# An attention and expert-routing kernel on one core: 64x64 products throughout the attention rounds, a new order of each round, and routing constants loaded two rounds earlier

## The chip, the cores and the metric

The kernel runs on one core of one Trainium2 chip. The metric is the device time of one execution in microseconds (us). TensorE is the matrix engine (PE in the profile; PEld is its loading of weights), VectorE is DVE, ScalarE is ACT, GpSimd is POOL, and SyncE (SP) issues most transfers.

## What is computed

For 8 batches and 8 heads, causal attention over 576 positions with a window of 128, head width 64 and a bias that falls linearly with distance; the result, transposed to 4608 tokens of 512 numbers, goes through a layer of 8 experts. Each token goes to one expert, in order of all the gate's logits, and each expert takes 576.

```python
scores = scale * np.matmul(q, k.transpose(0, 1, 3, 2))
mask = (rel >= 0) & (rel < window)
scores = np.where(mask, scores + bias[None], -1000000000.0)
attn = softmax(scores)                       # by row
x = (attn @ v).transpose(0, 2, 1, 3).reshape(4608, 512)
logits = x @ w_gate                          # one expert a token, 576 tokens an expert
out[mask] = np.maximum(x[mask] @ w1[e], 0.0) @ w2[e]
```

## The kernel before, in words

**Pairs and tiles.** The attention works on 32 pairs of heads (8 batches x 4 pairs, NPAIRS). The two heads of a pair lie on partitions 0 to 63 and 64 to 127. The 576 positions are nine blocks of 64. Tiles 0 to 3 hold two query blocks each; the block that is left over, the ninth, is put together for an even and the following odd pair and is called tile 4. A query block meets at most three key blocks, so a tile's scores are up to 192 columns wide.

**Rounds.** `attention` (L42) runs 32 rounds and a tail. What a round does, and in which order, is written out by hand in ROUND (L33), a list of words: a letter for the step, one for the tile (or half, or head), and which pair it serves, counted back from the round's number. `M21-0` is the minimum for tile 2, head 1 of this round's pair; `T3-2` the transposes of tile 3 of the pair two rounds back. The first round has a list of its own (ROUND0), and so has the end (TAIL, L38). Every instruction of these steps is kept in this order on its engine (`put`), so each engine walks its own part of the list in order, and waits when a step's input or buffer is not ready.

**The steps**, and their engines:

- S (`scores`, L127), TensorE: q times k, in two halves: units 2 and 3 (S0), and 0, 1 and 4 (S1). A head works on its own half of the array's rows. For tiles 1 to 4 each product is 64x64 (head h, query block r: four quarters of the array). Tile 0 is written as one product of 64x128 for each head (L150), since both its blocks see the same keys. The scores land in one of two buffers (`ps_s`, two copies).
- M (`least`, L157), VectorE: adds the bias, takes the row minimum of the negated scores. E (`exps`, L169), ScalarE: the exponential with its row sum.
- T (`turn`, L184), TensorE: transposes of 128x128 into one of two banks (`ps_t`). P (`turned`, L197): copies the bank to SBUF: ScalarE for tiles 1 and 2, VectorE for 0 and 3 (L210).
- A (`av`, L213), TensorE: probabilities times v, 64x64 products, into the tile x (`ps_x`, one copy). X (`copy_out`, L247): the two halves of x to the tile xT, one on VectorE and one on ScalarE, by the parity of the pair (L253).
- N (`natural`, L271), TensorE: turns xT back to natural order and forms the gate's logits in the same product (64 columns of identity and 8 of gate weights, 72). For each tile and head one product of 64x128 (L281), eight in all; in every second round the ninth block adds four of 64x64. Float32 products are two instructions each.
- L (`logit_shares`), D1 and D0 (`divide`), VectorE: scale by the reciprocal sums, which G (`sums`, GpSimd) and I (`inverse`, L262, VectorE) made. In the last two pairs D is done by ScalarE in sixteen small products (L326).
- V (`load_v`), Q (`load`, L63: the q and k of the pair two rounds ahead, behind the last product issued before it) and Z (`store`), SyncE.
- R1 to R3 (`route`, L410): slots in which one step at a time of the routing that can be done early is put on VectorE (and a few products on TensorE). They run the generators in `router.steps` in order; the first one there is `load_consts`.

**The constants.** In round 5 (CONST_AT, L479), where Q is done, the kernel starts `load_consts` (L430): a transfer of 337.5 KB into craw. The following R1 puts the first cast of it (to c_ones) on VectorE.

**After the attention** come the first routing phase and, expert by expert, two layers of products whose weights are loaded, split in two parts and multiplied; the other routing phases run beside them.

Of the kernel before, what the change touches and what calls it, by code (L numbers as in the profile page):

```python
# [5 lines left out]
F32 = mybir.dt.float32  # L6
# [10 lines left out]
E, DM, F, N = 8, 512, 1024, 4608  # L17
CAP = N // E
NP = H // 2
# [3 lines left out]
QKW, BMW, XW, GW = 1152, 1408, 72, 8  # L23
# [5 lines left out]
def parts(words):  # L29
    return [(w[0], w[1:-2], -int(w[-2:])) for w in words.split()]  # L30


ROUND = parts("""S1-0 V-1 Q+2 G-2 M00-0 M11-0 S0-0 E11-1 T0-2 E21-1 E10-1 M21-0 T1-2 E00-1 E20-1 P1-2 P0-2 A-3 R1-3 M40-0 M31-0 M41-0 M01-0  # L33
E30-1 X1-3 T3-2 E01-1 T2-2 X0-3 I-2 M10-0 R2-3 M30-0 M20-0 E40-0 E41-0 R3-3 P3-2 N-3 L-3 D1-3 E31-0 P2-2 D0-3 Z-3""")

ROUND0 = parts("S0-0 S1-0 Q+2 M20-0 E20-0 M30-0 E30-0 M21-0 E21-0 M31-0 E31-0 M00-0 E00-0 M10-0 E10-0 M01-0 E01-0 M11-0 E11-0")

TAIL = [parts("""V-1 E21-1 G-2 E30-1 E01-1 T0-2 T3-2 P3-2 E10-1 P0-2 E00-1 A-3 R1-3 T2-2 X1-3 X0-3 E20-1 T3-1 R2-3 R1-3 R2-3 N-3 R3-3 P3-1 D0-3 P2-2 T1-2  # L38
E11-1 G-1 P1-2 T2-1 D1-3 Z-3 T1-1 L-3 P2-1 T0-1 A-2 R1-2 P1-1 I-2 I-1 P0-1 R2-2 R3-2 X1-2 X0-2 R1-2 R2-2 A-1 X1-1 X0-1 N-2 L-2 N-1 L-1 D0-2 D1-2 Z-2 D1-1 D0-1 Z-1""")]


def attention(tc, pools, qk_in, v_in, rel_in, C, x_dram, L_sb, router):  # L42

    nc = tc.nc
    sb, ps_s, ps_t, ps_x = (pools[k] for k in ("attn", "ps_s", "ps_t", "ps_x"))
    ident, wn = C["ident"], C["wn"]
    state, bm, batch, late, done, made, next_time = {}, {}, {}, [], set(), [], []
    hs = [slice(64 * h, 64 * h + 64) for h in range(2)]
    HR = [(h, r) for r in range(2) for h in range(2)]
# [4 lines left out]
    def mm(out, w, a, start=True, stop=True):  # L54
        i = nc.tensor.matmul(out, w, a, start=start, stop=stop, skip_group_check=True)  # L55
        put(i)
        made[:] = [i]
# [5 lines left out]
    def load(n):  # L63

        if n < NPAIRS:
            b, p = divmod(n, NP)
            t = sb.tile([128, QKW], F32, name="qk", bufs=3)
            i = nc.sync.dma_start(t, qk_in[b, p])
            put(i)
            if n > 2:  # L70
                tc.add_manual_dep(i.ins, made[0].ins.name, AFTER, reason="one pair a round")
            state[n] = dict(q=t[:, 0:576], k=t[:, 576:1152])
# [36 lines left out]
    def keys(n, t, r):  # L109

        par = n // NP % 2
        qb = par + 2 * t + r if t < 4 else 8 - 8 * par
        if t == 0:
            return qb, 0, qb + 1
        return qb, max(0, qb - 2), min(3, qb + 1)
# [11 lines left out]
    def scores(n, half):  # L127
        half = int(half)
        st = state[n]
        q, k = st["q"], st["k"]  # L130
        if "u" not in st:
            st["u"] = sb.tile([128, 1792], F32, name="u", bufs=4)
            st["mn"] = sb.tile([128, 10], F32, name="mn", bufs=4)
            st["sm"] = sb.tile([128, 10], F32, name="sm", bufs=6)
        if half and n == 0:
            s = [bank() for _ in range(2)]
        else:
            two = banks(ps_x if half and n == 1 else ps_s)
            s = [two[:, 512 * h:512 * h + 512] for h in range(2)]
        st["s", half] = s  # L140
        for t in UNITS[half]:
            if t == 4 and n % 2 == 0:
                continue
            m, c = unit(n, t)[0:2]
            w = 64 * m
            if t == 0:

                qb = keys(n, 0, 0)[0]
                for h in range(2):
                    mm(s[h][:, c:c + w], q[hs[h], 64 * qb:64 * qb + 128], k[hs[h], 0:w])  # L150
                continue
            for h, r in HR:
                one = state[n - 1 + r] if t == 4 else st
                qb, kb, _ = keys(n, t, r)
                mm(s[h][hs[r], c:c + w], one["q"][hs[h], 64 * qb:64 * qb + 64], one["k"][hs[h], 64 * kb:64 * kb + w])
# [41 lines left out]
    def turned(n, t):  # L197
        t = int(t)
        st = state[n]
        if "PT" not in st:  # L200
            st["PT"] = sb.tile([128, 2048], F32, name="PT", bufs=3)
        if nines(n, t):
            c, w, dims = 0, 512, ()
        elif t:
            c, w, dims = 0, 192, ((256, 2),)
        elif n // NP % 2:
            c, w, dims = 64, 384, ()
        else:
            c, w, dims = 128, 128, ((192, 2),)
        copy = nc.scalar.copy if t in (1, 2) else nc.vector.tensor_copy  # L210
        put(copy(steps(st["PT"][:, 512 * t + c:512 * t + c + w], *dims), steps(st["pt", t][:, c:c + w], *dims)))  # L211

    def av(n):  # L213
# [33 lines left out]
    def copy_out(n, i):  # L247
        st = state[n]
        i = int(i)
        if "xT" not in st:  # L250
            st["xT"] = sb.tile([128, 640], F32, name="xT", bufs=3)
        w = 256 if i or not n else 384 if n == NPAIRS - 1 else 320
        copy = nc.vector.tensor_copy if n % 2 != i else nc.scalar.copy  # L253
        put(copy(st["xT"][:, 384 * i:384 * i + w], st["x"][:, 512 * i:512 * i + w]))  # L254

    def sums(n):
# [4 lines left out]

    def inverse(n):  # L262
        t = 4 + n % 2
        s = state[n]["rs"] = sb.tile([128, 5, 2], F32, name="rs", bufs=3)
        put(nc.vector.reciprocal(s[:, 0:t], state[n]["sd"][:, 0:2 * t].rearrange("q (t h) -> q t h", h=2)))

    def nine(n):
# [3 lines left out]
    def natural(n, which):  # L271


        st = state[n]
        N = st["N"] = banks(ps_s if n == NPAIRS - 1 else ps_x)
        xT = st["xT"]
        for t in range(4):
            g = t // 2
            o = 384 * g + 128 * (t % 2)
            for c in range(2):  # L280
                mm(N[:, 512 * c + XW * t:512 * c + XW * t + XW], xT[hs[c], o:o + 128], wn[hs[c], n % NP, g, :])  # L281
        k = nine(n)
        if k is not None:
            for c, r in HR:
                a = xT[hs[c], 256 + 64 * r:320 + 64 * r] if k == n else state[n - 1 + r]["xT"][hs[c], 256:320]
                mm(N[hs[r], 512 * c + 4 * XW:512 * c + 5 * XW], a, wn[hs[c], (k - 1 + r) % NP, 0, :])
# [130 lines left out]
    put(nc.scalar.copy(wn[hs[1], :, :, 0:64].rearrange("k p g c -> k (p g) c"), bc(ident[hs[1], 64:128].unsqueeze(1), [64, 2 * NP, 64])))  # L417
    for n in range(NPAIRS + len(TAIL)):
        if n == 1:
            wg = pools["pp"].tile([128, NP, 2, GW], F32, name="wg")  # L420
            nc.sync.dma_start(wg, C["wg_in"].rearrange("k (p o e) -> k p o e", p=NP, o=2))
        if n == 2:
            put(nc.scalar.copy(wn[:, :, :, 64:XW], wg))
        if 0 < n < NP:
            biases(n)
        for what, which, back in ROUND0 if n == 0 else ROUND if n < NPAIRS else TAIL[n - NPAIRS]:
            k = n - back
            if what == "Q":
                load(k)
                if n == CONST_AT:  # L430
                    router.steps.append(load_consts(tc, pools["c"], C["cst_in"], C, router.nc.vector))
                    next(router.steps[0])
            elif 0 <= k < NPAIRS and not (what in "ME" and ((what, which, k) in done or which[0] == "4" and k % 2 == 0)):
                done.add((what, which, k))
                if what in alone:
                    alone[what](k)
                else:
                    work[what](k, which)
        if n == 0:

            z = C["zero"].bitcast(F32)
            for i in range(IDLE):
                put(nc.tensor.matmul(C["idle"][hs[i % 2], 0:64], z[hs[0], 0:64], z[hs[0], 0:64], start=True, stop=True,
                                     skip_group_check=True))
# [34 lines left out]
CONST_AT = 5  # L479
# [731 lines left out]
def load_consts(tc, pool, cst, C, eng):  # L1211
    nc = tc.nc
    n = sum(w for _, w, _ in CONSTS)
    raw = pool.tile([128, n], F32, name="craw")
    tc.keep_in_program_order(nc.sync.dma_start(raw, cst))
    yield "hold"
    o = 0
    for k, w, dt in CONSTS:
        r = raw[:, o:o + w]
        if dt == F32:  # L1220
            C[k] = r
        else:
            if dt == BF:
                t = pool.tile([128, w], BF, name="c_" + k)
                eng.tensor_copy(t, r)
            else:
                t = pool.tile([128, w, dt], BF, name="c_" + k)
                eng.tensor_copy(t, bc(r.unsqueeze(2), [128, w, dt]))
            C[k] = t
            yield 0  # L1230
        o += w
# [170 lines left out]
```

## Time and profile before

| | us |
|---|---|
| three runs | 695.52, 696.99, 697.02 |
| their median | 696.99 |
| profiled execution, its own time | 698.88 |
| profiled execution, span of the core | 697.0 |
| TensorE's mean granted clock over the span | 0.973 of full speed |

The profile's times run from the span's start. Rounds begin where the scores begin, here by the pieces of the chain: round 5 at 29.28, round 6 at 43.64, round 7 at 52.27, round 31 at 202.52; at 228.80 the first product of the routing count that has to wait for all of the attention starts. An instruction of TensorE is listed with the time it takes from start to end; several overlap, so a group's length is not the sum of its members'. In a row of the timeline, the idle time of the engine before it and what ended it stand in brackets.

### The profile page before, as it was taken

What the parts mean: (1) busy time and instruction counts of PE and PEld (TensorE: products, weight loads), DVE (VectorE), ACT (ScalarE), POOL (GpSimd) and SP (SyncE); (2) the same over time, 40 slices, a digit from 0 to 9 for tenths busy, and PEclk for the clock granted to TensorE, in tenths of its full rate; (3) what the DMA queues carried; (4) which work ended last, traced back from release to release, by engine and by line L of the source; (5) the groups of instructions that cost most, each with busy time, mean ns of one, the idle gap of its engine ahead of it and who ended that gap; (6) DMA issues with size and microseconds to landing.
All of it is one profiled execution on the core that took longest, in us unless ns stands there. A gap on an engine that the chain in (4) does not pass through costs nothing.

```text
span 697.0 us, 17694 instructions
## 1 busy us (share of the span) xinstructions
PE 654.8 (94%) x6691; PEld 562.6 (81%) x6692; DVE 466.3 (67%) x1959; ACT 375.6 (54%) x1062; POOL 112.9 (16%) x183
## 2 busy tenths in 40 slices
PE   8969999999997499999999999999999999999995
PEld 5748878778776279889879878988988988988985
DVE  5648788788887789977849778794774724523310
ACT  6847888878874153433324526645645655644210
POOL 4001110110100020331412214014014014011011
PEclk9979999999999599999999999999999999999999
DMA  7426567556542360733614755555545565531001
GB/s 238 150 95 197 168 196 228 174 181 218 164 137 58 98 221 30 271 107 121 205 45 161 204 114 161 158 130 162 154 127 157 147 145 156 153 82 38 1 24 49
DMA packets 60637, 98.02 MB, mean 141 GB/s; under 512 B 27904, under 2 KB 39296, under 8 KB 60544
## 3 DMA queue, kind: packets, MB, share of 16 engines
q1 hardware_dynamic: 54656, 77.92, 37.4%
q0 software_dynamic: 5888, 18.88, 8.2%
q8 instruction: 55, 0.90, 0.5%
q14 instruction: 38, 0.31, 0.1%
HBM read 72.01 MB, written 18.87 MB: 130 GB/s over the span
## 4 chain that ended last, share of the span: by engine, by line
PE 79%; DVE 8%; ACT 3%; issue 3%; DMA 3%; another core or an unknown queue 1%; SPq 0%; POOL 0%; POOLq 0%; DVEq 0%; ACTq 0%
PE ph L1140 24%; PE x L55 12%; PE po L1168 10%; PE po L1169 10%; PE po L1171 8%; PE s L55 7%; PE pt L192 4%; DVE hl L1048 2%; DVE xT L254 2%; ACT xT L254 1%; DMA raw<-in_w_dram 1%; DMA craw<-in_cst_dram 1%; DVE hlo L1150 1%; PE m L686 1%
## 5 line engine op out<-in xcount | busy, mean ns | idle before, releaser
L1140 PE MATMUL ph<-xh,hl 128*128 128x288 f32 (+2 forms) x1024 | 190.4, 300 | 0.5
L1140 PEld LDWEIGHTS ph<-xh,hl 128*128 128x128 f32 x1024 | 155.9, 190 | 3.0 <-issue 1.8
L1168 PE MATMUL po<-hl,hh 128*128 128x512 f32 (+1 forms) x328 | 128.3, 391 | 0.0
L1169 PE MATMUL po<-hl,hh 128*128 128x512 f32 (+1 forms) x328 | 126.2, 385 | 0.0
L174 ACT ACTIVATE u<-u,mn 128x192 f32<-128x192 f32 (+2 forms) x288 | 124.5, 436 | 2.0 <-DVE mn L165 2.0
L1140 PE MATMUL ph<-xl,hl 128*128 128x288 f32 (+2 forms) x512 | 116.2, 299 | 0.0
L1145 ACT ACTIVATE hh<-ph 128x288 fp32r<-128x288 f32 (+2 forms) x128 | 46.6, 409 | 106.4 <-PE ph L1140 91.9
L1171 PE MATMUL po<-hl,hlo 128*128 128x512 f32 (+1 forms) x264 | 101.3, 384 | 0.0
L1048 DVE TENSOR_TENSOR hl<-raw,hl 128x512 fp32r<-128x512 f32 x128 | 85.2, 684 | 21.8 <-ACT hl L1046 21.7
L1180 POOL DMA_INDIRECT out_dram<-o,idx x40 | 41.0, 1024 | 279.9 <-ACT o L1175 212.4
L1140 PEld LDWEIGHTS ph<-xl,hl 128*128 128x128 f32 x512 | 84.7, 190 | 0.2 <-DVE xl L1119 0.2
L165 DVE CUSTOM_DVE_ANT_0 u<-s,bm 128x192 f32<-128x192 f32 (+2 forms) x278 | 80.4, 333 | 4.0 <-PE s L55 3.1
L1046 ACT CAST hl<-raw 128x1024 fp32r<-128x1024 f32 x64 | 66.1, 1051 | 27.2 <-DMA raw<-in_w_dram 19.5
L1168 PEld LDWEIGHTS po<-hl,hh 128*128 128x128 f32 x328 | 61.8, 188 | 11.2
L1169 PEld LDWEIGHTS po<-hl,hh 128*128 128x128 f32 x328 | 61.7, 188 | 11.3
L1150 DVE SCALAR_TENSOR_TENSOR hlo<-ph,hh 128x288 fp32r<-128x288 f32 (+2 forms) x128 | 49.2, 417 | 31.3 <-ACT hh L1145 30.5
L1175 ACT COPY o<-po 128x512 f32<-128x512 f32 (+1 forms) x33 | 18.9, 574 | 91.2 <-PE po L1171 72.3
L192 PE MATMUL pt<-ident_sb,u 128*128 128x128 f32 x368 | 57.1, 285 | 1.5 <-ACT PT L211 1.0
L1171 PEld LDWEIGHTS po<-hl,hlo 128*128 128x128 f32 x264 | 49.6, 188 | 9.9
L55 PE MATMUL s<-qk 64*64 64x192 f32 (+2 forms) x992 | 56.2, 330 | 1.6 <-DVE mn L165 1.6
L174 ACT ACTIVATION_READ_ACCUMULATOR u<-u,mn 128x1 f32 x288 | 55.1, 191 | 0.0
L55 PE MATMUL x<-wn_sb,xT 64*128 64x72 f32 (+1 forms) x616 | 39.9, 278 | 12.8 <-ACT xT L254 7.9
(261 smaller groups left out, 864.5 us busy)
## 6 DMA issues: line engine op xcount, KB each, us to landing
raw<-in_w_dram SPq DMA_DIRECT2D x64, 512.0 KB, 4.5
qk<-in_qk_dram SPq DMA_DIRECT2D x32, 576.0 KB, 5.3
v<-in_v_dram SPq DMA_DIRECT2D x32, 288.0 KB, 3.5
x<-xb SPq DMA_DIRECT2D x14, 512.0 KB
x<-xb SPq DMA_DIRECT2D x16, 64.0 KB
x<-xb SPq DMA_DIRECT2D x4, 256.0 KB, 2.3
g<-x,idx POOLq DMA_INDIRECT x40
out_dram<-o,idx POOLq DMA_INDIRECT x40
```

The source lines that it names most:

```text
L55: i = nc.tensor.matmul(out, w, a, start=start, stop=stop, skip_group_check=True)
L165: put(nc.vector.tensor_tensor_reduce(out=weights(n, t, h), in0=s[h][:, c:c + 64 * m].rearrange("q (j k) -> q j k", k=64), in1=bm[n % NP][: ...
L174: put(nc.scalar.activation(u, u, AF.Exp, bias=st["mn"][:, i:i + 1], scale=-1.0, accum_out=st["sm"][:, i:i + 1]))
L192: put(nc.tensor.transpose(steps(ps[:, c:c + 64], (w, 2)), u[:, o + 128 * j:o + 128 * j + 128], ident))
L1046: self.last = nc.scalar.copy(hl[:, 0, :], raw)
L1048: nc.vector.tensor_tensor(hl[:, 1, c:c + 512], raw[:, c:c + 512], hl[:, 0, c:c + 512].bitcast(F32), ALU.subtract)
L1140: nc.tensor.matmul(pp[t], w[:, a, j, fo:fo + 128], x[:, j, cut[t]:cut[t + 1]], start=(i == 0), stop=(i == 11))
L1145: self.acted = nc.scalar.activation(o, pp[t], AF.Relu)
L1150: nc.vector.scalar_tensor_tensor(d, pp[t][:, c0:c1], 0.0, o[:, c0:c1].bitcast(F32), ALU.max, ALU.subtract)
L1168: nc.tensor.matmul(out, a, wh, start=(f == 0), stop=False)
L1169: nc.tensor.matmul(out, a, wl, start=False, stop=(f == 7 and t == 4))
L1171: nc.tensor.matmul(out, hl[:, f, 128 * t:128 * t + 128], wh, start=False, stop=(f == 7))
```

## The change

It does five things. The eight 64x128 products of N become sixteen of 64x64, in fours that use the four quarters of the array. Tile 0's scores are done like the other tiles', in 64x64 products. ROUND and TAIL are written anew: S0 follows S1 at once; the exponentials of tile 3 and the copy P0 move to the next round; I serves the pair three rounds back; T goes 3, 1, then A, then 2, 0; X0 comes right behind A and R1, and X1 near the end. The copies P1, P2 and X0 are VectorE's and P0, P3 and X1 ScalarE's, in all rounds. The constants' transfer is issued in round 3, while the steps that cast them still enter the list in round 5. The reciprocals' tile has six copies in place of three.

```diff
-ROUND = parts("""S1-0 V-1 Q+2 G-2 M00-0 M11-0 S0-0 E11-1 T0-2 E21-1 E10-1 M21-0 T1-2 E00-1 E20-1 P1-2 P0-2 A-3 R1-3 M40-0 M31-0 M41-0 M01-0
-E30-1 X1-3 T3-2 E01-1 T2-2 X0-3 I-2 M10-0 R2-3 M30-0 M20-0 E40-0 E41-0 R3-3 P3-2 N-3 L-3 D1-3 E31-0 P2-2 D0-3 Z-3""")
+ROUND = parts("""E30-2 S1-0 V-1 Q+2 S0-0 I-3 M41-0 E31-2 G-2 M01-0 P0-3 M21-0 T3-2 M20-0 E21-1 M10-0 E20-1 E10-1 T1-2 E11-1 M00-0 P1-2 M11-0 M40-0 P3-2 A-3 R1-3 X0-3
+E41-0 E40-1 T2-2 E00-1 M31-0 R2-3 M30-0 E01-0 T0-2 P2-2 X1-3 R3-3 N-3 D1-3 L-3 D0-3 Z-3""")
-TAIL = [parts("""V-1 E21-1 G-2 E30-1 E01-1 T0-2 T3-2 P3-2 E10-1 P0-2 E00-1 A-3 R1-3 T2-2 X1-3 X0-3 E20-1 T3-1 R2-3 R1-3 R2-3 N-3 R3-3 P3-1 D0-3 P2-2 T1-2
-E11-1 G-1 P1-2 T2-1 D1-3 Z-3 T1-1 L-3 P2-1 T0-1 A-2 R1-2 P1-1 I-2 I-1 P0-1 R2-2 R3-2 X1-2 X0-2 R1-2 R2-2 A-1 X1-1 X0-1 N-2 L-2 N-1 L-1 D0-2 D1-2 Z-2 D1-1 D0-1 Z-1""")]
+TAIL = [parts("""V-1 E11-1 E00-1 P0-3 T0-1 E21-1 T0-2 P0-1 P0-2 E20-1 T1-2 E31-2 T2-2 E30-2 G-2 P2-2 E30-1 E31-1 P1-2 I-3 A-3 R1-3 X1-3 T2-1 R2-3 T3-2 E40-1 E10-1 G-1
+R1-3 X0-3 P2-1 R2-3 I-2 N-3 R3-3 D0-3 P3-2 L-3 T3-1 D1-3 Z-3 T1-1 A-2 R1-2 P3-1 P1-1 R2-2 X0-2 R3-2 I-1 R1-2 X1-2 R2-2 A-1 X0-1 N-2 X1-1 N-1 L-2 L-1
+D0-2 D1-2 Z-2 D1-1 D0-1 Z-1""")]
+
+ON_VECTOR = {(0, "P1"), (1, "P1"), (0, "P2"), (1, "P2"), (0, "X0"), (1, "X0")}
...
-            if t == 0:
-
-                qb = keys(n, 0, 0)[0]
-                for h in range(2):
-                    mm(s[h][:, c:c + w], q[hs[h], 64 * qb:64 * qb + 128], k[hs[h], 0:w])
-                continue
...
-        copy = nc.scalar.copy if t in (1, 2) else nc.vector.tensor_copy
+        copy = nc.vector.tensor_copy if (n % 2, f"P{t}") in ON_VECTOR else nc.scalar.copy
...
-        copy = nc.vector.tensor_copy if n % 2 != i else nc.scalar.copy
+        copy = nc.vector.tensor_copy if (n % 2, "X%d" % i) in ON_VECTOR else nc.scalar.copy
...
-        s = state[n]["rs"] = sb.tile([128, 5, 2], F32, name="rs", bufs=3)
+        s = state[n]["rs"] = sb.tile([128, 5, 2], F32, name="rs", bufs=6)
...
-            o = 384 * g + 128 * (t % 2)
-            for c in range(2):
-                mm(N[:, 512 * c + XW * t:512 * c + XW * t + XW], xT[hs[c], o:o + 128], wn[hs[c], n % NP, g, :])
+            for c, r in HR:
+                o = 384 * g + 128 * (t % 2) + 64 * r
+                mm(N[hs[r], 512 * c + XW * t:512 * c + XW * t + XW], xT[hs[c], o:o + 64], wn[hs[c], n % NP, g, :])
...
+                if n == CONST_AT - 2:
+                    consts = load_consts(tc, pools["c"], C["cst_in"], C, router.nc.vector)
+                    next(consts)
                 if n == CONST_AT:
-                    router.steps.append(load_consts(tc, pools["c"], C["cst_in"], C, router.nc.vector))
-                    next(router.steps[0])
+                    router.steps.append(consts)
```

## Rows read from the trace of the kernel before

**Rows 1.** The page's chain that ended last, share of the span by engine.

```profile
PE 79%; DVE 8%; ACT 3%; issue 3%; DMA 3%; another core or an unknown queue 1%; SPq 0%; POOL 0%; POOLq 0%; DVEq 0%; ACTq 0%
```

**Rows 2.** Windows by stage: busy us (and count) of PE, PEld, DVE, ACT, POOL; PEclk; DMA.

```profile
29.28:43.64 14.36, 7.41 (x129) 6.03 (x126) 5.54 (x31) 6.07 (x26) 0.20 (x1) 0.83 0.45 144
43.64:52.27 8.63, 8.40 (x111) 6.28 (x112) 5.03 (x27) 4.29 (x18) 0.20 (x1) 0.69 0.22 70
52.27:202.52 150.25, 146.20 (x2751) 119.44 (x2751) 125.08 (x666) 124.10 (x507) 14.58 (x60) 1.00 0.58 188
202.52:228.80 26.28, 19.55 (x382) 16.22 (x380) 19.42 (x91) 14.51 (x60) 2.07 (x8) 0.96 0.27 80
```

**Rows 3.** Timeline of SyncE's issues, 14 to 36 us: start, length, instruction.

```profile
18.46 0.33 SPq L68 DMA_DIRECT2D qk<-in_qk_dram  x1
...
24.33 0.33 SPq L68 DMA_DIRECT2D qk<-in_qk_dram  x1
...
32.28 0.45 SPq L1215 DMA_DIRECT2D craw<-in_cst_dram  x1
```

**Rows 4.** Timeline of all engines, 26 to 44 us.

```profile
39.30 0.23 DVE L521 CAST c_ones<-craw 128x128 bf16<-128x128 f32 x1 [7.56 <-DMA craw<-in_cst_dram]
...
41.22 2.43 PE L55 MATMUL x<-wn_sb,xT 64*128 64x72 f32 x24 [6.96 <-ACT xT L254]
```

**Rows 5.** Timeline of TensorE in rounds 14 and 15, 101.8 to 121.5 us.

```profile
108.54 1.63 PE L55 MATMUL s<-qk 64*128 64x128 f32 x28
110.10 0.88 PE L192 MATMUL pt<-ident_sb,u 128*128 128x128 f32 x6
...
113.49 1.11 PE L55 MATMUL x<-wn_sb,xT 64*128 64x72 f32 x16 [0.24 <-DVE xT L254]
114.44 1.90 PE L55 MATMUL s<-qk 64*128 64x128 f32 x36
...
119.65 1.40 PE L55 MATMUL x<-wn_sb,xT 64*128 64x72 f32 x24
120.98 0.81 PE L55 MATMUL s<-qk 64*128 64x128 f32 x8
```

**Rows 6.** TensorE's 64x64 groups in narrow windows; then durations by source line, min/median/max ns.

```profile
121.40 1.21 PE L55 MATMUL s<-qk 64*64 64x192 f32 x24
...
120.70 0.36 PE L55 MATMUL x<-wn_sb,xT 64*64 64x72 f32 x8
...
L55 PE MATMUL s<-qk x992: 216/323/683, 5.4 to 203.8; 64*64 64x192 f32 x163, 64*128 64x128 f32 x12, 64*128 64x192 f32 x12, 64*64 64x64 f32 x12
...
L55 PE MATMUL x<-wn_sb,xT x616: 222/272/482, 22.3 to 223.5; 64*128 64x72 f32 x124, 64*64 64x72 f32 x30
```

**Rows 7.** VectorE by line and shape, 52.27 to 202.52: count, busy us, mean ns, idle before.

```profile
L211 DVE COPY PT<-pt 128x384 f32<-128x384 f32 x25 | 13.9, 554 | 1.3
L211 DVE COPY PT<-pt 128x512 f32<-128x512 f32 x12 | 8.2, 684 | 0.0
...
L254 DVE COPY xT<-x 128x320 f32<-128x320 f32 x12 | 5.9, 492 | 15.0 <-ACT xT L254 15.0
...
L211 DVE COPY PT<-pt 128x256 f32<-128x256 f32 x12 | 5.1, 424 | 0.0
```

**Rows 8.** Timeline of VectorE behind natural order of round 13, with a ninth block.

```profile
108.68 0.28 DVE L299 TENSOR_TENSOR Lp<-x,rs 128x64 f32<-128x64 f32 x1
...
109.76 0.28 DVE L165 CUSTOM_DVE_ANT_0 u<-s,bm 128x128 f32<-128x128 f32 x1
...
109.97 0.35 DVE L165 CUSTOM_DVE_ANT_0 u<-s,bm 128x192 f32<-128x192 f32 x1
110.24 0.08 DVE L165 DVE_READ_ACCUMULATOR2_ANT mn<- 128x1 f32 x1
```

**Rows 9.** Timeline of ScalarE and TensorE at the end of the tail.

```profile
224.54 1.75 ACT L326 ACTIVATE xb<-x,rs 128x64 f32<-128x64 f32 x8 [2.00 <-PE x L55]
...
228.80 0.31 PE L521 MATMUL m<-OH,ind 128*128 128x16 bf16 x5 [3.75 <-ACT xb L326]
```

## The prediction

> **What bounds the kernel now.** I read the chain that ended last first [rows 1]: TensorE carries 79% of it. The windows by stage [rows 2] say where that leaves room. From 228.80 on (routing, then the experts' layers) nothing is edited, so those 697.0 - 228.8 = 468.2 us stay. The attention before falls into four pieces: round 5 (14.36 us), round 6 (8.63), the 24 rounds from 7 to 30 (150.25, so 6.26 each), and round 31 with the tail (26.28). In the 24 rounds TensorE is busy 146.20 of 150.25, VectorE 125.08 and ScalarE 124.10. So TensorE sets the pace, but with only 17% of room on each of the other two: what it gains can be kept only until one of them, or a ring through all three, takes over.
>
> **The constants.** Their load is issued at 32.28 [rows 3], in round 5, and the cast that reads them stood on VectorE's ordered queue until 39.30, 7.56 us idle; with that queue the copies of xT stood, and TensorE idled 6.96 us until 41.22 [rows 4]. Afterwards the granted clock is 0.69 over round 6 (full before, half for part of it) [rows 2]. Rounds 5 and 6 took 14.36 + 8.63 = 22.99 us where two ordinary ones take 12.52: the load costs **10.5 us**. Issued in round 3 it stands on SyncE's queue behind the q/k load of 18.46; between it and the next q/k load, at 24.33 [rows 3], there is one v load, wanted three rounds later, which it delays by its own 0.45 us of issue. From issue to cast it took 39.30 - 32.28 = 7.02 us; from 18.8 it would land at about 26, and the cast is not wanted before round 5's A, at some 32. I take all of the 10.5; its bounds are 0 (still late) and 10.5.
>
> **Natural order in 64x64.** In round 14 the sixteen 64x128 instructions take 113.49 to 114.44, 0.95 us until the scores begin; in round 15, with eight 64x64 ones of the ninth block behind, 119.65 to 120.98, 1.33 [rows 5]. Sixteen in 1.11 us, less the 0.27 that one lasts [rows 6], start as eight pairs 0.12 us apart. The change makes thirty-two of them, in eight fours on the four quarters of the array. What a four costs is bounded by two rows [rows 6]: the ninth block's eight instructions of the same 72 columns, two fours, all start within 0.14 us (0.36 less the 0.22 that a short one lasts), entering the mode included; six fours of 192 columns start within 1.21 - 0.32 = 0.89 us, five steps of 0.17, also with the entry, which by columns is 0.065 for 72. I take 0.065, since of the ninth block only one step, the one with the entry, can be seen, and 0.05 for the entry: 8 x 0.065 + 0.05 = 0.57 without a ninth block, 10 x 0.065 + 0.05 = 0.70 with one. That saves 0.38 in even rounds and 0.63 in odd ones. If a four cost 0.113 (the 0.14 less start offsets), nothing would be saved in even rounds and 0.15 in odd ones.
>
> **Tile 0's scores.** Today they and the change of mode take 120.98 to 121.40, 0.42 us [rows 5, 6]. Two fours of 128 columns are 2 x 0.17 x 128/192 = 0.23. Saved: about 0.2, plus the entry that is no longer paid twice, 0.23 in all.
>
> A rule of the Trainium skill speaks against this part: "TensorE: Matmul & The Clock Gate", section "Wait — 56ns, not 53.3ns?", has the starts of matmuls never closer than some 25 ns, however narrow; by it (an estimate) N would take 0.80 and 1.00 and the sum would end some 7 us higher, near 673. The rows disagree: the ninth block's eight start within 0.14 us, 0.02 each [rows 6].
>
> **A round of TensorE** then is: even (108.54 to 114.44 now, 5.90 [rows 5]): scores 1.56 - 0.23, transposes and A 110.10 to 113.49, 3.39, of which 0.24 is waiting for xT, natural 0.57: 5.29, or 5.05 without the wait. Odd (114.44 to 120.98, 6.54): 6.54 - 0.63 - 0.23 = 5.68, with 0.2 of waiting in it. The mean is 5.27 without waits.
>
> **The other engines.** Copies P1, P2 and X0 go to VectorE, P0, P3 and X1 to ScalarE. VectorE gives up 24 of 554 ns, 12 of 684 and 12 of 424, and 12 xT copies of 256 columns (priced as P's 256, 424 ns); it takes 36 of 554, 12 of 684 and 12 xT of 492 [rows 7]. That is +1.6 and +0.8 us over 24 rounds, so 125.08/24 + 0.1 = 5.31 us a round; ScalarE falls by about 0.08 from 5.17. VectorE's floor is now as high as TensorE's.
>
> **The ring.** In the new order VectorE's queue runs, once natural order has ended: L, D1 and D0 (at a round's end, so they overlap the next scores), I, the minima M up to M40, P1, R1, X0; ScalarE's X1 follows X0 (the two are in series today, the row of X0 waits 15.0 us for ScalarE's [rows 7]); then natural order again. For an odd round: natural 0.86 to its last end and 0.1 to L; L to the first M 109.76 - 108.68 = 1.08; I 0.13; eight M at 110.24 - 109.97 = 0.27 from start to start [rows 8], some narrower, 2.1; P1 0.55; a router step 0.1; X0 0.49, X1 0.37, three hops of 0.05: 5.9. An even one, with six M and no ninth block, 5.0, beneath its TensorE sum. So odd rounds become VectorE's (6.0 with slips), even ones stay TensorE's (5.2): **5.60 a round**, 0.66 less, times 24 is **15.8 us**. Bounds: 5.31 (22.8 us) and 5.95 (7.4).
>
> The other moves cost nothing on the path. E30 and E31 start a round later, but ScalarE has them done before the scores end, ahead of T3. P0 comes after them, and T1, which wants its bank, stands behind all scores; if ScalarE ran a microsecond late, T3 and T1 would wait that long. S0 right behind S1 wants M31 and M30 of the round before, which precede P2. G on GpSimd and I move together; GpSimd is idle. The larger ring of rs tiles is memory only. The q/k load stays behind S1.
>
> **Early rounds and tail.** Rounds 5 and 6, once ordinary, gain 0.66 each; rounds 3 and 4 are partly ScalarE's, 0.3 each: 1.9. Round 31 gains 0.66. In the tail two natural-order groups of 1.3 us and one of 0.95 shrink by 1.6 in all. The closing products of ScalarE now start 2.0 us after its last copy, at 224.54, and the routing count waits for their end, 228.80 [rows 9]; with N-2 ahead of X1-1 they start about 1 us sooner. Against this stand three more exponentials left for the tail, 3 x 0.44. I take 0.66 + 1.6 + 0.7 = **3.0**, bounds 1 and 5.
>
> **Sum.** 10.5 + 15.8 + 1.9 + 3.0 = 31.2. The profiled execution took 698.88 us (span 697.0), 1.9 above the median of 696.99; 698.88 - 31.2 = 667.7, and as a median **665.8**.
>
> **Rivals.**
> - *VectorE's floor is reached*: the ring slips into the even rounds' slack and rounds take 5.31: 7.0 less, 659. For it: the order differs from round to round only by two minima. Against: an in-order queue at its floor has no idle at all. 0.13.
> - *The small products keep a distance by instruction, not by four.* The nearest rows give 0.02 an instruction (0.14/7, the ninth block) and 0.039 (0.89/23, the scores, 192 columns) [rows 6]: thirty-two take 0.64 to 1.25 us. In the middle, 0.03, N is 0.96 and 1.2, as with fours of 0.113: 0.4 to 0.5 more in each round, on TensorE and in the ring, rounds of about 5.95 and a smaller tail: 677. Against: in the ninth block the step between the fours holds the entry too. 0.06. (Such a distance is what the section of the Trainium skill named above states.)
> - *The ring runs later than its sum*: ScalarE's E41, E40, E00 and E01 stand before X1; if the M's they follow are late, N waits and rounds take 5.9 to 6.0: 674. For it: ScalarE at 5.09 of 5.60 us has little room left. Against: in the sum X1 is wanted 1.5 us after their last M. 0.07.
> - *The constants still come late*, because three loads at once are slower than today's: all 10.5 lost, 676. For it: the load shares the queues with q/k and v; against: 5 us of cover. 0.03.
> - *Slower: the ring pays full durations.* If each M cost 0.35 + 0.08 [rows 8] with no overlap and each hop 0.2, the ring would be about 7.9 in odd and 6.4 in even rounds, 7.2: 0.94 over today, 22.5 more in 24 rounds against 13.5 saved elsewhere: 706. It decides once rounds exceed some 6.8. Against: the M's start 0.27 apart in the rows. 0.02.
>
> My forecast has 0.69. What a measurement of this kernel can tell from no change is about 0.3%, 2.1 us; only the last rival, and half a percent of mishap, lie at or above that: faster 0.97, same 0.01, slower 0.02. The forecast's own range is 661 to 671; the rivals on both sides stretch it to 657 and 677.
>
> **What would show it.** The cast of c_ones has no wait, and the clock is 1.00 in rounds 5 and 6. Natural order is a row of x32 or x40 that lasts 0.8 to 0.95. No s matmul has the form 64*128. Rounds 7 to 30 take 134 us, odd ones near 6.0, even near 5.2, VectorE busy some 95%, and TensorE waits for X1 before N in odd rounds alone. It is wrong if the rounds stay over 5.9, if a four takes 0.1, or if the stage after the count changes length by over 2 us.

## The result and the profile after

The changed kernel takes **668.11 us** (median of 4 runs, 666.87 to 668.95); the kernel before took 697.0 beside it (4 runs, 695.52 to 697.4). The ratio is 0.9588, 95% interval 0.9567 to 0.9609. The forecast was 665.8, the range 657 to 677. The profiled execution took 668.95 us, with a span of 666.8.

The windows by stage of the kernel after answer to [rows 2]: rounds 5 and 6, rounds 7 to 30, round 31 with the tail, and everything from the routing count on.

```profile
29.04:34.88 5.84, 5.62 (x153) 4.72 (x149) 5.55 (x30) 5.17 (x24) 0.20 (x1) 1.00 0.67 220
34.88:40.27 5.39, 5.16 (x136) 4.27 (x131) 5.20 (x29) 4.73 (x21) 0.20 (x1) 1.00 0.54 193
40.27:175.36 135.09, 128.15 (x3230) 106.95 (x3225) 125.38 (x666) 119.58 (x505) 14.59 (x60) 1.00 0.65 209
175.36:199.77 24.41, 17.22 (x461) 14.59 (x454) 18.79 (x91) 16.08 (x67) 2.21 (x9) 0.97 0.29 87
199.77:666.80 467.03, 446.17 (x2916) 395.62 (x2916) 292.83 (x1036) 204.14 (x366) 91.63 (x89) 0.98 0.42 127
```

Rounds 5 and 6 fell from 14.36 and 8.63 us to 5.84 and 5.39, at the full clock. The 24 rounds fell from 150.25 to 135.09 us, 5.63 each: odd ones last 5.81 to 5.98, even ones 5.25 or 5.39, but for round 30 with 6.06 (6.79 before). TensorE is busy in 95% of them, VectorE in 93%. The stage behind the count is 1.2 us shorter. The chain that ended last has moved only by a little towards VectorE [rows 1]:

```profile
PE 78%; DVE 13%; ACT 3%; issue 2%; another core or an unknown queue 1%; DMA 1%; SPq 0%; POOL 0%; POOLq 0%; DVEq 0%; ACTq 0%
```

SyncE's issues in round 3 (start, length, instruction), for [rows 3], and VectorE's timeline in round 5, for [rows 4]:

```profile
18.89 0.33 SPq L71 DMA_DIRECT2D qk<-in_qk_dram  x1
19.26 1.14 SPq L1214 DMA_DIRECT2D craw<-in_cst_dram  x1
20.44 0.43 SPq L81 DMA_DIRECT2D v<-in_v_dram  x1
...
24.36 0.33 SPq L71 DMA_DIRECT2D qk<-in_qk_dram  x1
```

```profile
32.66 0.22 DVE L520 CAST c_ones<-craw 128x128 bf16<-128x128 f32 x1
```

The cast has no wait in front of it, and the next q/k load leaves at 24.36 as it did at 24.33.

The v load behind the constants' issue leaves 20.44 - 18.89 = 1.55 us after the q/k load in front of it; it was 0.37 in the kernel before.

Now two rounds, an even and an odd one, in the timeline of all engines: A, the copies X0 (VectorE) and X1 (ScalarE), N, and the scores that follow. The brackets tell how long the engine was idle in front, and what ended it.

```profile
104.01 1.55 PE L58 MATMUL x<-PT,v 64*64 64x192 f32 x48
...
105.65 0.49 DVE L251 COPY xT<-x 128x320 f32<-128x320 f32 x1 [0.28 <-PE x L58]
...
106.17 0.37 ACT L251 COPY xT<-x 128x256 f32<-128x256 f32 x1 [0.42 <-DVE xT L251]
...
106.60 0.73 PE L58 MATMUL x<-wn_sb,xT 64*64 64x72 f32 x32 [0.34 <-ACT xT L251]
...
107.15 1.70 PE L58 MATMUL s<-qk 64*64 64x128 f32 x40
...
111.44 0.49 DVE L251 COPY xT<-x 128x320 f32<-128x320 f32 x1 [0.22 <-PE x L58]
...
111.97 0.37 ACT L251 COPY xT<-x 128x256 f32<-128x256 f32 x1 [0.64 <-DVE xT L251]
...
112.39 0.86 PE L58 MATMUL x<-wn_sb,xT 64*64 64x72 f32 x40 [0.19 <-ACT xT L251]
```

Natural order takes 107.15 - 106.60 = 0.55 us until the scores begin, where sixteen 64x128 products took 0.95 [rows 5]. Inside a four the instructions start 0.007 us apart; from one four to the next it is 0.063, and 0.11 for the first step. In front of it TensorE waits for X1 in the even round too. X1 begins 0.03 us behind the end of X0 (105.65 + 0.49), and X0 itself waited for the end of A. So A, X0, X1 and N stand one behind the other, and VectorE had idled 0.28 and 0.22 us before X0: it was ready before TensorE was. X0 starts 0.05 to 0.09 us behind the end of A in 20 of the 24 rounds; in rounds 13, 21 and 29 it starts 0.21 to 0.22 behind it with no idle time of VectorE in front, so there VectorE was the later one.

The waits up to the count (engine and what it waited for: us in total, times, longest):

```profile
ACT xT L251 <- DVE xT L251: 16.4, 27, 0.8
...
PE x L58 <- ACT xT L251: 8.8, 29, 0.8
DVE xT L251 <- PE x L58: 4.6, 19, 0.4
```

TensorE's groups by shape in rounds 7 to 30 (count, busy us, mean ns, idle before) show that no product with 64*128 is left, for scores or natural order:

```profile
L58 PE MATMUL s<-qk 64*64 64x192 f32 x721 | 34.6, 323 | 0.0
...
L58 PE MATMUL x<-wn_sb,xT 64*64 64x72 f32 x864 | 19.0, 228 | 6.9 <-ACT xT L251 6.9
L58 PE MATMUL s<-qk 64*64 64x128 f32 x96 | 4.8, 269 | 0.0
```

The end of the tail, in the timeline of all engines, answers to [rows 9]:

```profile
194.52 0.96 PE L58 MATMUL s<-wn_sb,xT 64*64 64x72 f32 x40
195.53 1.74 ACT L323 ACTIVATE xb<-x,rs 128x64 f32<-128x64 f32 x8 [0.70 <-PE s L58]
...
199.77 0.31 PE L520 MATMUL m<-OH,ind 128*128 128x16 bf16 x5 [4.29 <-ACT xb L323]
```

ScalarE's closing products wait 0.70 us where they waited 2.00; the count still waits for their end.

### The profile page after: what moved, and what is told of

Its sections match the earlier page's. It is cut to its first block, busy times and chain, and to the rows that moved or that the text cites. A ratio compares the mean times of both kernels' runs of the same rounds, so it can differ in the third digit from the quotient of the medians.

```text
span 666.8 us, 19019 instructions
## 1 busy us (share of the span) xinstructions
PE 627.3 (94%) x7331; PEld 544.2 (82%) x7332; DVE 466.9 (70%) x1959; ACT 370.9 (56%) x1062; POOL 116.2 (17%) x183
## 4 chain that ended last, share of the span: by engine, by line
PE 78%; DVE 13%; ACT 3%; issue 2%; another core or an unknown queue 1%; DMA 1%; SPq 0%; POOL 0%; POOLq 0%; DVEq 0%; ACTq 0%
PE ph L1139 25%; PE po L1167 10%; PE x L58 10%; PE po L1168 10%; PE po L1170 8%; PE s L58 6%; PE pt L189 3%; DVE xT L251 2%; DVE hl L1047 2%; ACT xT L251 2%; DVE u L162 1%; DVE hlo L1149 1%; PE pg L1080 1%; PE m L685 1%
## 5 line engine op out<-in xcount | busy, mean ns | idle before, releaser
L1179 POOL DMA_INDIRECT out_dram<-o,idx x40 | 42.9, 1073 | 276.5 <-ACT o L1174 214.8
L1056 POOL DMA_INDIRECT g<-x,idx x40 | 42.6, 1066 | 63.0 <-DVE L L520 24.6
L189 PEld LDWEIGHTS pt<-ident_sb,u 128*128 128x128 f32 x368 | 39.8, 140 | 13.0 <-issue 8.5
```

The source lines that it names most:

```text
L189: put(nc.tensor.transpose(steps(ps[:, c:c + 64], (w, 2)), u[:, o + 128 * j:o + 128 * j + 128], ident))
```

## The experiments

A table first, for reading the sections below; all stages are from the profiled executions, in us, "rounds" being 7 to 30 and "tail" round 31 to the count. Each stage is counted from the first score product of its first round (the changed kernel's rounds from 40.09 to 175.36, so 135.27, where the window above has 135.09). Before and b_const, whose rounds 7 to 30 hold the same work, agree there within 0.01 us. The kernel before ran beside each group of runs on the same chip.

| kernel | median | before beside it | ratio, 95% interval | rounds 3 to 6 | rounds | tail |
|---|---|---|---|---|---|---|
| before | 697.0 | | | 35.00 | 150.23 | 26.47 |
| after | 668.11 | 697.0 | 0.9588 (0.9567 to 0.9609) | 22.36 | 135.27 | 24.42 |
| b_const | 687.11 | 696.47 | 0.9871 (0.983 to 0.9912) | 24.52 | 150.22 | 26.47 |
| b_nat | 682.55 | 696.47 | 0.9808 (0.9756 to 0.986) | 31.71 | 140.94 | 25.80 |
| b_tile0 | 689.54 | 696.47 | 0.9897 (0.9856 to 0.9939) | 33.57 | 145.31 | 26.29 |
| b_order | 697.65 | 696.47 | 1.0015 (0.9992 to 1.0038) | 33.09 | 152.93 | 25.65 |
| a_oldorder | 665.15 | 692.46 | 0.9605 (0.9574 to 0.9636) | 22.06 | 134.21 | 25.57 |
| a_dve | 666.06 | 692.46 | 0.9628 (0.9589 to 0.9667) | 22.40 | 137.58 | 24.43 |
| a_dve2 | 663.74 | 692.46 | 0.959 (0.9552 to 0.9629) | 22.35 | 135.74 | 24.44 |
| a_pe | 672.57 | 692.46 | 0.9713 (0.9682 to 0.9745) | 23.66 | 142.24 | 24.43 |
| a_lsplit | 666.52 | 696.15 | 0.9581 (0.9548 to 0.9614) | 22.36 | 135.62 | 24.50 |
| a_two | 661.02 | 696.15 | 0.9498 (0.9466 to 0.953) | 21.80 | 132.50 | 23.89 |
| a_two_old | 661.82 | 696.15 | 0.9503 (0.9466 to 0.9539) | 21.17 | 133.28 | 24.83 |

The chips differ by some 4 us, and the long stage behind the count varies from one execution to the next (461 to 468 us in these profiles, with nothing edited there), so medians are compared within a group, and parts of a round by stage.

### One part of the change at a time, in the kernel before

**b_const**: the constants alone.

```diff
+                if n == CONST_AT - 2:
+                    consts = load_consts(tc, pools["c"], C["cst_in"], C, router.nc.vector)
+                    next(consts)
...
-                    router.steps.append(load_consts(tc, pools["c"], C["cst_in"], C, router.nc.vector))
-                    next(router.steps[0])
+                    router.steps.append(consts)
```

> The kernel before with one edit: the constants' transfer is issued in round 3 and cast in round 5 as before. Theory (the load was late by its own flight, and all of that and of the half clock behind it comes back): 10.5 us less, 686 to 687, the cast of c_ones without a wait, the clock 1.00 over rounds 5 and 6. Rival (three transfers at once are slower, the cast still waits): less than 5 us back, 692 to 697, with a wait left in front of the cast.

Measured: rounds 3 to 6 take 35.00 - 24.52 = 10.5 us less, and the rounds behind do not change at all. The windows of rounds 3 to 6 and 7 to 30 of this kernel:

```profile
17.64:42.16 24.52, 24.07 (x448) 19.61 (x449) 19.51 (x105) 21.94 (x91) 1.01 (x5) 1.00 0.55 176
42.16:192.38 150.22, 146.16 (x2753) 119.41 (x2753) 125.05 (x668) 124.07 (x509) 14.58 (x60) 1.00 0.59 188
```

The clock column is 1.00 where round 6 had 0.69 [rows 2]: with the idle time gone, the half-clock stretch behind it is gone too. The median moved by 9.4 us; the difference to 10.5 lies within its interval.

**b_nat**: natural order alone in 64x64 products, as the change writes it.

```diff
-            for c in range(2):
-                mm(N[:, 512 * c + XW * t:512 * c + XW * t + XW], xT[hs[c], o:o + 128], wn[hs[c], n % NP, g, :])
+            for c, r in HR:
+                o = 384 * g + 128 * (t % 2) + 64 * r
+                mm(N[hs[r], 512 * c + XW * t:512 * c + XW * t + XW], xT[hs[c], o:o + 64], wn[hs[c], n % NP, g, :])
```

> The kernel before with one edit: natural order in sixteen 64x64 products in place of eight 64x128 ones. Theory (a four costs 0.065 us, and TensorE sets the pace of the rounds): natural order 0.6 to 0.75 us in place of 0.95 and 1.33, 0.33 less in even and 0.58 less in odd rounds, some 13 us in 29 rounds and the tail: 683 to 686. Rival (the small products keep a distance by instruction, 0.03 us): 0 to 3 us less, 694 to 697. Second rival (the shorter products end in a longer wait for xT): natural order as short as the theory says and the rounds as long as before, 694 to 697.

Measured: 9.3 us less in the 24 rounds, 13.9 in the median. TensorE's timeline of two rounds:

```profile
100.71 0.85 PE L55 MATMUL x<-wn_sb,xT 64*64 64x72 f32 x40
101.50 1.63 PE L55 MATMUL s<-qk 64*128 64x128 f32 x28
...
106.45 0.73 PE L55 MATMUL x<-wn_sb,xT 64*64 64x72 f32 x32 [0.24 <-DVE xT L254]
107.11 1.95 PE L55 MATMUL s<-qk 64*128 64x128 f32 x36
```

From natural order to the scores it is 0.79 and 0.66 us here, 0.11 more than in the changed kernel (112.39 to its scores 0.68, and 0.55). a_oldorder (below), which keeps this kernel's order and has tile 0's scores in 64x64 too, has the 0.68 and 0.55 as well. The groups themselves last the same, 0.85 or 0.86 and 0.73. What differs is the next instruction: here the scores begin with tile 0's 64x128 product, so the shape changes behind N. **Going from 64x64 products to a 64x128 one cost 0.11 us.** That part of it is the longer weight load of the 64x128 product is not excluded by this pair.

**b_tile0**: tile 0's scores alone (the six lines with the 64x128 case are left out, so that tile 0 goes the way of the others).

> The kernel before with one edit: tile 0's scores in 64x64 products like the other tiles'. Theory (two fours in place of two pairs, one change of mode less a round): 0.2 us a round, 6 us in all, 690 to 692. Rival (scores are hidden behind the minima and exponentials that follow): below 2 us, 695 to 698.

Measured: 4.9 us less in the 24 rounds, 0.20 a round, and 6.9 in the median. Natural order, in even rounds, now takes 1.05 us until the scores where it took 0.95 [rows 5]:

```profile
109.83 1.11 PE L55 MATMUL x<-wn_sb,xT 64*128 64x72 f32 x16 [0.24 <-DVE xT L248]
110.88 1.75 PE L55 MATMUL s<-qk 64*64 64x128 f32 x40
```

N is as before, and what follows it is a 64x64 product and no longer a 64x128 one: the change of shape costs 0.10 us in this direction too, where the weight load that follows is the shorter one (0.13 us against 0.19). In odd rounds, where the ninth block ends N in 64x64 products and no change is left behind it, the scores begin 1.22 us after N in place of 1.33.

**b_order**: the new ROUND and TAIL, the new share of the copies and the six rs tiles, without any of the three parts above.

> The kernel before with the new ROUND and TAIL, the new share of the copies between VectorE and ScalarE and six copies of the reciprocals, but the old products and the old place of the constants' transfer. Theory (TensorE sets the pace and its work is the same, so an order can win only its waits for xT, 0.15 to 0.3 us a round, and the new one has the copies X0 and X1 in series right before natural order too): 693 to 700, no change to speak of. Rival (the order is what makes the kernel faster): 689 or less.

Measured: no difference that can be told in the median (ratio 1.0015, 0.9992 to 1.0038); by stage the 24 rounds are 2.7 us longer, the tail 0.8 and rounds 3 to 6, the constants' stall among them, 1.9 shorter. The waits of this kernel up to the count, the constants' stall in them:

```profile
ACT xT L257 <- DVE xT L257: 23.4, 28, 5.7
PEld x L58 <- ACT xT L257: 20.6, 30, 5.5
PE x L58 <- ACT xT L257: 13.5, 29, 5.2
```

The four medians add up to 9.4 + 13.9 + 6.9 - 1.2 = 29.0 us, the whole change gave 28.9; as each has an interval of 1.6 to 3.6 us to either side, that says little. In the 24 rounds they do not add up: 9.3 + 4.9 - 2.7 = 11.5 against 15.0. a_oldorder (the next section) splits the 3.5 that the parts give only together: the two kinds of products in the old order give 150.23 - 134.21 = 16.0 where they gave 14.2 one by one, 1.8 more, and the new order costs 1.1 beside them and not 2.7, 1.6 more. A cause for the 1.8 can be read from the rows above: the change of shape between N and the scores is gone in all rounds only when both are 64x64. From N to the scores an even round saves 0.40 us with both, and 0.29 - 0.10 = 0.19 with each alone, 2.5 us in twelve rounds. That is more than 1.8; TensorE's idle time in the rounds rose by 1.7 in a_oldorder, from 4.0 to 5.7 us, and it did not in b_nat and b_tile0.

### The order taken out of the changed kernel

**a_oldorder**: the reverse of b_order, the old ROUND, TAIL, share of copies and three rs tiles with the small products and the early constants kept.

> The changed kernel with the old ROUND and TAIL, the old share of the copies and three copies of the reciprocals: the products and the constants' transfer alone. If the gains of the three single edits simply add (9.4, 13.9 and 6.9 us), 666 to 668, as the changed kernel itself: the order is then worth nothing here either. Rival (with TensorE's work 0.7 us shorter a round, the old order leaves waits that the new one was made to remove): 672 or more.

Measured: the 24 rounds take 134.21 us, 1.1 less than in the changed kernel, and the tail 25.57, 1.1 more; the ratios, 0.9605 and 0.9588, cannot be told apart. So no gain from the new order can be told here. The copies' waits in this kernel:

```profile
PE x L55 <- DVE xT L248: 4.1, 13, 0.5
...
PE x L55 <- ACT xT L248: 1.6, 4, 0.9
```

In the old order TensorE waits 5.7 us for the copies, in the new one 9.9 (8.8 for X1, 1.1 for X0).

### What the path of a round is made of

**a_dve**, **a_dve2**: an addition on VectorE that nobody reads, in 26 rounds, behind I (ahead of all minima), or behind M30 (behind X0 and the minima that follow it).

```diff
+        if 3 <= n < NPAIRS - 3:
+            more = sb.tile([128, 256], F32, name="more", bufs=1)
+            put(nc.vector.tensor_tensor(more, rel[:, 0:256], rel[:, 128:384], ALU.add))
```

> The changed kernel with one more VectorE instruction in 26 rounds, an addition of 128x256 numbers right behind I, ahead of the minima and so inside the ring from natural order to X0. The ring as predicted (VectorE sets the odd rounds, TensorE the even ones): about 0.3 us more in 13 odd rounds, 3.5 to 4.5 in all, 671.5 to 673. Rival (X0 waits 0.2 to 0.3 us for A in the changed kernel's trace, so the ring has slack in both kinds of round and A, X0, X1 and natural order are what is in series): 0 to 1.5 us, 668 to 669.5.

> The same additional instruction placed behind the minimum M30, after X0 and so outside the ring. If VectorE's whole time is the limit (125.4 of 135.1 us busy, 0.4 idle a round): the idle time is used up and little more, 0 to 2 us, 668 to 670; if it is at its floor already, the full 0.3 a round, 8 us, 676. If the ring is the limit: 0 to 1.

**a_pe**: tile 3's scores written twice in 26 rounds, eight 64x64 instructions more; the numbers do not change.

```diff
-        for t in UNITS[half]:
+        for t in UNITS[half] + ((3,) if not half and 3 <= n < NPAIRS - 3 else ()):
```

> The changed kernel with tile 3's score products done twice in 26 rounds, two more fours of 192 columns (the same numbers written again), 0.33 us. If TensorE is in the path of every round: 0.33 in each, 8 to 9 us, 676 to 677. The ring as predicted (odd rounds are VectorE's, with 0.4 us of TensorE waiting in them): even rounds alone, 4 to 5 us, 672 to 673.5.

VectorE's addition in a_dve by shape (count, busy us, mean ns), and below it the windows of rounds 7 to 30 of a_dve, a_dve2 and a_pe:

```profile
L265 DVE TENSOR_TENSOR more<-rel_sb 128x256 f32<-128x256 f32 x26 | 10.7, 410 | 0.0
```

```profile
39.57:177.15 137.58, 128.31 (x3242) 107.08 (x3238) 132.29 (x690) 119.82 (x505) 16.92 (x60) 1.00 0.63 205
```

```profile
39.35:175.09 135.74, 128.50 (x3241) 107.12 (x3237) 131.46 (x689) 119.82 (x505) 14.61 (x60) 1.00 0.64 208
```

```profile
40.85:183.09 142.24, 135.45 (x3418) 113.90 (x3414) 127.20 (x666) 121.58 (x505) 14.66 (x60) 1.00 0.61 199
```

The changed kernel has 135.27 us there, with VectorE busy for 125.56 and TensorE for 128.32 (40.09 to 175.36). In a_dve VectorE's busy time rose by 132.29 - 125.56 = 6.7 us and 2.3 were paid, a third, between the two expectations; behind M30 it rose by 5.9 and 0.5 was paid. TensorE's rose by 135.45 - 128.32 = 7.1 and 7.0 were paid; 22 of the 26 rounds with more work lie in the window, and they paid 0.32 or 0.33 each, odd and even, but for 13 and 21 (0.19 and 0.20) and 26 (0.42). Of a_dve's 2.3, rounds 13, 21 and 29 paid some 0.34 each, rounds 11, 19 and 27 nothing, the other odd ones 0.09 to 0.24, and of the even ones 14, 22 and 30 0.10 to 0.13. TensorE is in the path of nearly every round; VectorE's work in front of X0 binds fully in three odd ones, the rounds in which X0 was late already, and is taken up wholly or in part in the others.

### The two copies side by side

X1 waits for X0 though it reads another half of the tile x. Both halves lie in one tile of two banks. In **a_two** A and N write two tiles of one bank each; each step then takes its half.

```diff
     def banks(pool):
-        return pool.tile([128, 1024], F32, name="x" if pool is ps_x else "s")
+        if pool is ps_x:
+            return [pool.tile([128, 512], F32, name="x%d" % i) for i in range(2)]
...
-        put(copy(st["xT"][:, 384 * i:384 * i + w], st["x"][:, 512 * i:512 * i + w]))
+        put(copy(st["xT"][:, 384 * i:384 * i + w], st["x"][i][:, 0:w]))
```

An instruction can't read two tiles as one, so L becomes two instructions (as does the ninth block's part of L and D). **a_lsplit**, the control, is the changed kernel with L in two; **a_two_old** is a_two with the order, tail, copies' share and rs of the kernel before.

```diff
-        put(nc.vector.tensor_tensor(Lp[:, 0:4, :, 2 * p:2 * p + 2].rearrange("q t e c -> q c t e"), four,
-                                    bc(s[:, 0:4].rearrange("q t c -> q c t").unsqueeze(3), [128, 2, 4, 8]), ALU.mult))
+        for c in range(2):
+            put(nc.vector.tensor_tensor(Lp[:, 0:4, :, 2 * p + c], four[:, c], bc(s[:, 0:4, c].unsqueeze(2), [128, 4, 8]), ALU.mult))
```

> The changed kernel with the step L (the logit shares) as two VectorE instructions, one for each half of the channels, in place of one; nothing else. It is the control of the next run, which needs L in that form. Theory 1 (TensorE and the two copies X0 and X1 in series are in the path of every round, VectorE is only near it): L stands behind N and ahead of the next round's minima, some 0.1 to 0.2 us of extra VectorE work is taken up in most rounds; rounds 7 to 30 take 135.3 to 137.5 us. Theory 2 (VectorE's chain is in the path of every round): all of it is paid, 24 x 0.1 to 0.2 = 2.4 to 4.8 us, rounds 7 to 30 take 137.7 to 140 us.

> The changed kernel with the two-bank tile that A and N are written to made two tiles of one bank each, so that ScalarE's X1 no longer waits for VectorE's X0; L is two instructions as in the run beside it, and the part of each even round's L and D that takes the ninth blocks is two as well. Theory 1 (A, X0, X1 and N stand in series in every round; the wait of 0.19 to 0.34 us for X1 in front of N is a real part of the round): X1 runs beside X0, N's wait for X1 is gone, and at most a remainder for X0 is left; 24 x 0.27 = 6.5 us less the extra VectorE work; rounds 7 to 30 take 129 to 133 us, 3 to 6 us less than in the run beside it, and VectorE's share in them rises to 96% or more (125.4 us of work before, and the extra work on top). Theory 2 (VectorE's chain through the minima sets the odd rounds, and TensorE's wait in front of N is slack that comes back elsewhere): the wait moves to S or to another step, and rounds 7 to 30 stay within 2 us of the run beside it.

> The same two tiles, with the order of the round, the tail, the engine of the copies and the depth of rs of the kernel before (the two small products and the early constants stay). Theory 1: with the old order N waited 4.1 us in all for VectorE's copy and 1.6 for ScalarE's, so less is to be had from copies side by side: 2 to 4 us of 134.2 less the extra VectorE work, rounds 7 to 30 take 131 to 135 us. If so, the new order is worth something only where the copies run side by side. Theory 2 (the copies are not in the path): within 1 us of 134.2 plus the extra work of L, 134 to 138 us.

The windows of rounds 7 to 30 of a_lsplit, and then of a_two:

```profile
39.29:174.91 135.62, 128.65 (x3241) 107.15 (x3237) 126.89 (x690) 119.78 (x505) 14.58 (x60) 1.00 0.65 208
```

```profile
38.49:170.99 132.50, 130.28 (x3239) 108.65 (x3234) 128.24 (x716) 121.01 (x503) 14.43 (x60) 1.00 0.66 213
```

The second instruction of L cost 126.89 - 125.56 = 1.3 us of VectorE and 0.35 of the rounds. With two tiles the rounds are 3.1 us shorter than that, TensorE is busy in 98% of them and VectorE in 97%, and the median falls from 666.52 to **661.02**, under both kernels. Two rounds of a_two in the timeline of all engines:

```profile
114.04 0.37 ACT L253 COPY xT<-x 128x256 f32<-128x256 f32 x1
114.11 0.49 DVE L253 COPY xT<-x 128x320 f32<-128x320 f32 x1
...
114.65 0.73 PE L58 MATMUL x<-wn_sb,xT 64*64 64x72 f32 x32
...
119.39 0.37 ACT L253 COPY xT<-x 128x256 f32<-128x256 f32 x1
...
119.71 0.48 DVE L253 COPY xT<-x 128x320 f32<-128x320 f32 x1
...
120.24 0.85 PE L58 MATMUL x<-wn_sb,xT 64*64 64x72 f32 x40
```

X0 and X1 overlap or change places, and N begins with no idle time of TensorE in front. In the rounds TensorE's idle time fell from 135.62 - 128.65 = 7.0 us to 132.50 - 130.28 = 2.2, and its busy time rose by 1.6; 3.1 is what is left. Why the busy time rose is not settled; that the weight loads of T wait for the exponentials for 4.7 us in these rounds (0.5 in a_lsplit), and those of N for X0 for 4.3, would fit it.

a_two_old's rounds are 0.9 us shorter than a_oldorder's (134.21 to 133.28), with the second L in them. They hold one stall that no other run shows at this size (a_two stops in the same place for 0.39): four instructions into natural order of round 26 TensorE stopped for 1.74 us, for nothing that the profile shows, as this row of its timeline has it:

```profile
147.90 0.65 PE L55 MATMUL x<-wn_sb,xT 64*64 64x72 f32 x26 [1.74 <-issue]
```

Without it the rounds would have taken some 131.5 (an estimate). So with the copies side by side, too, neither the medians (661.02 and 661.82) nor the rounds give the new order an advantage. Which of the two is better there stays open; the two tiles help either.

## Why the prediction was right, and where it was not

**The sum.** 31.2 us were forecast, 28.9 came; by the profiled executions 698.88 - 668.95 = 29.9.

**The constants**: forecast 10.5 of bounds 0 to 10.5, measured 10.5 by stage in b_const; in the changed kernel, too, the cast has no wait. The issue at 19.26 was put at 18.8, the transfer was on time, and the v load behind it moved by 1.2 us, where its own issue of 0.45 was reckoned with: the issue took 1.14. No wait for v shows in the waits up to the count.

**Natural order**: forecast 0.57 and 0.70 us to the scores, measured 0.55 and 0.68. The step of a four from the columns of the scores (0.065) and the 0.05 for the entry held: 0.063 and 0.05 in the trace. The rival of a distance by instruction fell, as the starts inside a four are 0.007 us apart. The Trainium skill, "TensorE: Matmul & The Clock Gate", section "Wait — 56ns, not 53.3ns?", has the starts of matmuls never closer than some 25 ns, by which (an estimate) the thirty-two would have taken 0.80 us. The trace disagrees for products in different quarters of the array.

**Tile 0's scores**: forecast 0.23 a round, measured 0.20 alone. The change of shape, taken at 0.05 here as in natural order, cost 0.11 from 64x64 to 64x128 (b_nat against a_oldorder) and 0.10 the other way (b_tile0).

**The rounds**: forecast 5.60 and 134 us, measured 5.63 and 135.1, odd 5.81 to 5.98 for 6.0, even 5.25 or 5.39 for 5.2. The numbers are near, and the reason was wrong. The step that failed is **the ring**, and with it "odd rounds become VectorE's". The ring's sum started each round at N's end and ran through L, D, I and the minima to X0. In the trace X0 waits for the end of A 19 times up to the count, 4.6 us in all, with VectorE done with what stands in front, 0.22 us of it in the odd round shown and 0.28 in the even one. Only rounds 13, 21 and 29 are VectorE's. In the other odd ones the ring is nearly as long as TensorE's way, so its sum gave nearly the right number by luck; a_dve shows that a third of an addition on it is paid, a_pe that nearly all of an addition on TensorE is. The prediction that TensorE waits for X1 in odd rounds alone was wrong with it: it waits 29 times, 8.8 us.

What stands in the place of the ring is TensorE's own round plus the two copies in series. The prediction saw that X1 follows X0, and priced it as a link of the ring; it took even rounds as 5.29 with a wait of 0.24 or 5.05 without. They were 5.25 to 5.39, with a wait of 0.23 or 0.34. The wait did not go in the new order, because X0 and X1 read one tile. a_two, in which they read two, took the wait away and 3.1 us of the rounds with it.

**"The other moves cost nothing"** was right for the median, but hid terms that nearly cancel: the new order costs 1.1 us in the 24 rounds with the small products (a_oldorder) and gives 1.15 in the tail; without them it costs 2.7 in the rounds (b_order).

**Early rounds and tail**: rounds 3 to 6 gained 12.6, 10.5 of it the constants', so 2.1 for 1.9. The tail gained 2.0 by the table, forecast 3.0. The step that was mis-sized is what the small products save there: 0.66 for round 31 and 1.6 for the three groups were expected, and a_oldorder, with the old tail, gained 26.47 - 25.57 = 0.9. The chain there runs through the copies and ScalarE more than through TensorE: a natural-order group of the tail, at 187.61, waited 1.07 us for VectorE's copy. The order gave 1.15 for the 0.7 expected; ScalarE's closing products did start earlier.

**The stage behind the count** changed by 1.2 us, within the bound of 2 that was set, and within what it varies by itself.

## What to carry to other kernels

Where two engines copy two halves of one tile out of PSUM, look in the timeline for the second copy starting at the end of the first: one tile for both orders them, and two tiles of a bank each let them run side by side. Two engines at 93% and 95% do not say which one is in the path; adding 0.3 to 0.4 us to each in turn, and seeing what part is paid, does. Before a reordering is priced, read who waits ahead of the step it is meant to feed: here the order of forty steps gave nothing that the median shows, and the shapes of the products gave some 20 us (13.9 and 6.9 alone).

## What the runs showed of the hardware

64x64 products of 72 columns on the four quarters of the array started 0.007 us apart inside a four and 0.063 from four to four, thirty-two in 0.55 us, while sixteen 64x128 products took 0.95. Going from 64x64 products to a 64x128 one cost 0.11 us more than staying, a fifth of what a whole natural-order group now takes, and going back 0.10. And the half-clock stretch behind the 7 us of idle time in round 5 [rows 2, 4] did not occur once that idle time was gone (1.00 in rounds 3 to 6 of b_const).
